# Attention in pairs of chunks: joint scores, transposes and value products ahead of two expert layers

## The chip, the core and the metric

The kernel runs on one core of one Trainium2 chip. The metric is the device time of one execution in microseconds, the median of several runs. Before the change it is 778.92 us (three runs, 778.86 to 779.86).

The engines are called as the profile calls them: PE (TensorE matmuls) and PEld (its weight loads), DVE (VectorE), ACT (ScalarE), POOL (GpSimd) and SP (SyncE, which here only issues transfers).

## What is computed

Three layers follow each other. q, k and v are 4 batches of 8 heads, 576 positions, 64 columns each.

```python
# attention over a window of 64 positions, 4 x 8 heads
scores = (1/8) * q @ k.T ; where not (0 <= i - j < 64): -1e9
x = softmax(scores) @ v                      # 2304 tokens x 512
# first MLP: 512 -> 2048 -> 512
h = x @ w_in
g = maximum(h, 0) + log1p(exp(-abs(h)))      # softplus
x = g @ w_out
# second MLP: 8 experts, each token takes the one with the largest logit
logits = x @ w_gate + modality_bias[modality_id]
out[tokens of e] = gate * (maximum(x @ w1[e], 0) @ w2[e])
```

## The kernel before

**Blocks, steps and chunks.** The 2304 tokens are cut into 6 blocks of 384. The first MLP runs over a block in 16 steps. Step f multiplies the block by the f-th 128 columns of w_in (`mm1`, lines 238 to 240: twelve matmuls, since each number is held as a high and a low part, xh and xl, and three of the four products are made), makes the softplus of it on ACT, DVE and POOL (gh and gl, its high and low parts), and two steps later (LAG is 2) multiplies gh and gl by the f-th 128 rows of w_out (`mm2`, lines 267 to 269: nine matmuls into px, three tiles of PSUM). After a block's last step ACT copies px out (`r_evac`, line 367), and in the next block DVE makes the router's dot products of it (`r_dots`, line 356).

In block 0 the weights are decoded as well (`w_decode`, lines 222 to 228): each of sixteen weight tiles W0 to W15 arrives as 64-bit numbers and is turned into two fp32r halves by two ACT and five DVE operations, two steps ahead of its use.

**Attention.** A block has 6 chunks of 64 queries. The chunks of block 0 are done ahead of the first step. The attention of block b + 1 is laid into the steps of block b, chunk by chunk, by `attn_slots` (line 184): chunk i of a block has its scores in step 2i + 1, its normalisation in step 2i + 2, its transposes in step 2i + 3 and its value products in step 2i + 4; the loads for the next chunk are in step 2i. One chunk goes this way:
- `a_scores` (line 116): 8 score matmuls of 64 x 64 x 128 into `pss` (tag pS: one tile of two PSUM banks, of which one chunk fills half); DVE adds the mask and takes the maximum, ACT makes four exponentials with their sums. Chunks under 12 (BUSY) have their mask added by 8 more matmuls.
- `a_norm` (line 151): reciprocals on DVE, the product on POOL (ACT for chunks 6 to 11).
- `a_probs` (line 161): 4 transposes into `pp` (tag pA, one bank, one buffer), copied by ACT to `pT`.
- `a_av` (line 170): 8 value matmuls into `pav` (the same tag pA), then ACT copies the result to xh and DVE takes the rest as xl. The first `mm1` of the next block reads xh and xl of all six chunks.

**What sets the order.** The program is written in the order of the loop at line 738; a scheduler then places each engine's instructions by its own estimate of time, under the data dependencies and the tiles' buffers. So what stands in a row on PE is not what stands in a row in the code. SP's transfers wait in order: a chunk's v transfer waits until the value products of the chunk two before are done.

Of the kernel before, what the change touches and what calls it, by code (L numbers as in the profile page):

```python
# [34 lines left out]
def attention_moe_moe_kernel(ctx, tc, q, k, v, w_in, w_out, modality, w_gate, mod_bias, w1, w2, out):  # L35
# [51 lines left out]
    def diff(eng, out_, a, hi):  # L87
        eng.tensor_tensor(out_, a, hi.bitcast(F32), ALU.subtract)  # L88
# [6 lines left out]
    def half(j, z):  # L95
        return (j + z) % 2
# [18 lines left out]

    def a_scores(c, tags=None, s=None):
        w = at[c]
        win, n, qT, kT = w["win"], w["n"], w["q"], w["k"]
        if tags is None:
            both = ps.tile([P, 2, 4, P], F32, name="pss", tag="pS")  # L120
            parts = [both[:, :, 0:2, 0:n]]
            bank = [both[:, z, 0:2, 0:n] for z in range(2)]
        else:
            bank = [ps.tile([P, 2, P], F32, name=f"pss{z}", tag=tags[0], bufs=tags[1])[:, :, 0:n] for z in range(2)]
            parts = [x[:, None] for x in bank]
# [34 lines left out]

    def a_probs(c, tag="pA", bufs=1, pT=None):
        s, n = at[c].pop("s"), at[c]["n"]
        pp = ps.tile([P, NPR, P], F32, name="pp", tag=tag, bufs=bufs)
        for j in range(NPR):
            nc.tensor.transpose(pp[0:n, j, :], s[:, j, 0:n], ident)
        pT = sb.tile([P, NPR, P], F32, name="pT", bufs=1) if pT is None else pT
        nc.scalar.copy(pT[0:n], pp[0:n])
        at[c]["pT"] = pT

    def a_av(c, tag="pA"):  # L170
        pT, n, vr = at[c].pop("pT"), at[c]["n"], at[c]["vr"]
        if c % CPB == 0:
            xblk[c // CPB] = (sb.tile([P, KD, TB], F32R, name="xh"), sb.tile([P, KD, TB], F32R, name="xl"))
        xh, xl = xblk[c // CPB]
        col = slice((c % CPB) * C, (c % CPB + 1) * C)
        po = ps.tile([P, NPR, C], F32, name="pav", tag=tag)
        for j in range(NPR):
            for z in range(2):
                r = slice(z * C, (z + 1) * C)
                nc.tensor.matmul(po[r, j, :], vr[0:n, j * P + z * C:j * P + (z + 1) * C], pT[0:n, 2 * z + j // 2, half(j, z) * C:(half(j, z) + 1) * C], start=True, stop=True)  # L180
        nc.scalar.copy(xh[:, :, col], po)
        diff(nc.vector, xl[:, :, col], po, xh[:, :, col])

    def attn_slots(b):

        c0 = b * CPB
        slots = [[] for _ in range(16)]
        for i in range(CPB):
            c = c0 + i
            slots[2 * i + 1].append((0, a_scores, c))  # L190
            slots[2 * i + 2].append((0, a_norm, c))
            slots[2 * i + 3].append((1, a_probs, c))
            slots[2 * i + 4].append((1, a_av, c))
            if c + 1 < B * NCB:
                slots[2 * i].append((2, a_load, c + 1))
        return slots
# [505 lines left out]
    evs = [ev0[:, i * D:(i + 1) * D] for i in range(4)] + [ev1[:, i * D:(i + 1) * D] for i in range(2)]  # L702
    work = ev1[:, 2 * D:3 * D].rearrange("p (j f) -> p j f", j=NPR)

# [3 lines left out]

    for part, c in [('qk', 0), (0, 0), ('qk', 1), ('v', 0), (1, 0), ('qk', 2), ('v', 1), ('v', 2), ('v', 3), (0, 1), ('v', 4), ('v', 5), (1, 1), (0, 2), (1, 2), ('qk', 6), ('v', 6), (0, 3), (1, 3)]:
        if part in (0, 1):  # L710
# [6 lines left out]
        else:  # L717
            a_load(c, None, part)
    for i in range(CPB + 3):
        if i < CPB:  # L720
# [7 lines left out]
        if 2 <= i < CPB + 2:  # L728
            a_probs(i - 2, "ph", 2, work if i % 2 else None)
    steps = NB * NF  # L730
# [149 lines left out]
```

## Time and profile before

| | |
|---|---|
| median of three runs | 778.92 us |
| the profiled execution's own time | 781.15 us |
| its span, first to last instruction | 779.1 us |
| mean granted clock of TensorE | 0.978 |
| PE busy, share of the span | 735.8 us, 94% |
| PEld | 617.7 us, 79% |
| DVE | 448.2 us, 58% |
| ACT | 361.6 us, 46% |
| POOL | 236.4 us, 30% |

The span falls into a beginning up to about 58 us (transfers, the attention of block 0, the first decoded weights), the rest of block 0 to about 129 us, blocks 1 to 5 to about 527 us, and the experts after it. The shares of busy time are means over these. Matmuls are pipelined: their rows overlap, so the distance from one start to the next says what a matmul costs, and not the length of its row.

### The profile page before, as it was taken

What the parts mean: (1) busy time and instruction counts of PE and PEld (TensorE: products, weight loads), DVE (VectorE), ACT (ScalarE), POOL (GpSimd) and SP (SyncE); (2) the same over time, 40 slices, a digit from 0 to 9 for tenths busy, and PEclk for the clock granted to TensorE, in tenths of its full rate; (3) what the DMA queues carried; (4) which work ended last, traced back from release to release, by engine and by line L of the source; (5) the groups of instructions that cost most, each with busy time, mean ns of one, the idle gap of its engine ahead of it and who ended that gap; (6) DMA issues with size and microseconds to landing.
All of it is one profiled execution on the core that took longest, in us unless ns stands there. A gap on an engine that the chain in (4) does not pass through costs nothing. (4 is left out here: it accounts for less than half of the span.)

```text
span 779.1 us, 12784 instructions
## 1 busy us (share of the span) xinstructions
PE 735.8 (94%) x4527; PEld 617.7 (79%) x4527; DVE 448.2 (58%) x1049; ACT 361.6 (46%) x867; POOL 236.4 (30%) x268
## 2 busy tenths in 40 slices
PE   5669999999989999999999999999989999999995
PEld 4457788888878888888788889878778888888884
DVE  6999994894397336953794349753432322223243
ACT  5779875545454445455545434543122212222143
POOL 2000000234225222333234213551464344353311
PEclk9769999999999999999999999999999999999998
DMA  9866433301141112111411015042021111111100
GB/s 329 295 212 212 155 101 122 117 1 50 36 128 42 28 48 89 35 48 49 129 36 20 23 40 200 26 178 100 17 71 50 35 56 47 37 57 43 41 28 17
DMA packets 42266, 65.17 MB, mean 84 GB/s; under 512 B 12797, under 2 KB 25469, under 8 KB 42056
## 3 DMA queue, kind: packets, MB, share of 16 engines
q1 hardware_dynamic: 37656, 54.45, 21.4%
q0 software_dynamic: 4528, 9.74, 3.8%
q8 instruction: 37, 0.61, 0.3%
q14 instruction: 45, 0.37, 0.2%
HBM read 54.37 MB, written 10.06 MB: 83 GB/s over the span
## 5 line engine op out<-in xcount | busy, mean ns | idle before, releaser
L88 POOL TENSOR_TENSOR gl<-a,gh 128x384 fp32r<-128x384 f32 x80 | 89.3, 1117 | 176.6 <-ACT gh L254 112.2
L238 PE MATMUL ph<-xh,W 128*128 128x384 f32 x384 | 133.5, 350 | 7.6 <-DVE a L251 6.1
L239 PE MATMUL ph<-xl,W 128*128 128x384 f32 x384 | 131.3, 342 | 0.8 <-DVE xl L88 0.8
L240 PE MATMUL ph<-xh,W 128*128 128x384 f32 x384 | 131.0, 341 | 0.0
L267 PE MATMUL px<-W,gh 128*128 128x512 f32 x288 | 116.3, 404 | 0.0
L268 PE MATMUL px<-W,gh 128*128 128x512 f32 x288 | 114.9, 399 | 0.0
L269 PE MATMUL px<-W,gl 128*128 128x512 f32 x288 | 107.3, 401 | 0.8 <-POOL gl L88 0.8
L249 ACT ACTIVATE a<-a 128x384 f32<-128x384 f32 x80 | 42.0, 525 | 104.2 <-DVE a L248 104.1
L159 POOL TENSOR_TENSOR s<-s,sm 128x512 f32<-128x512 f32 (+1 forms) x24 | 26.0, 1082 | 199.3 <-DVE sm L154 173.9
L238 PEld LDWEIGHTS ph<-xh,W 128*128 128x128 f32 x384 | 72.7, 190 | 15.4 <-DVE a L251 8.1
L629 POOL DMA_INDIRECT gx<-x2s,pieces x76 | 73.6, 968 | 23.6 <-issue 14.0
L239 PEld LDWEIGHTS ph<-xl,W 128*128 128x128 f32 x384 | 72.8, 190 | 4.2 <-DVE xl L88 1.5
L248 DVE TENSOR_SCALAR a<-ph 128x384 int32<-128x384 int32 x80 | 44.1, 551 | 51.6 <-PE ph L240 48.8
L251 DVE SCALAR_TENSOR_TENSOR a<-ph,a 128x384 f32<-128x384 f32 x96 | 53.0, 552 | 35.7 <-ACT a L250 35.6
L240 PEld LDWEIGHTS ph<-xh,W 128*128 128x128 f32 x384 | 73.0, 190 | 0.2
L254 ACT CAST gh<-a 128x384 fp32r<-128x384 f32 x96 | 49.0, 512 | 47.3 <-DVE a L251 45.6
L269 PEld LDWEIGHTS px<-W,gl 128*128 128x128 f32 x288 | 53.1, 188 | 13.4 <-POOL gl L88 1.7
L658 PE MATMUL p<-w,x2h 128*128 128x512 f32 x152 | 62.3, 410 | 1.2 <-ACT x2h L644 1.2
L267 PEld LDWEIGHTS px<-W,gh 128*128 128x128 f32 x288 | 54.4, 189 | 10.7 <-issue 1.2
L268 PEld LDWEIGHTS px<-W,gh 128*128 128x128 f32 x288 | 54.5, 189 | 8.9 <-issue 0.3
L661 PE MATMUL p<-w,x2h 128*128 128x512 f32 x152 | 60.4, 397 | 0.0
L662 PE MATMUL p<-w,x2l 128*128 128x512 f32 x152 | 60.3, 398 | 0.0
(196 smaller groups left out, 1335.2 us busy)
## 6 DMA issues: line engine op xcount, KB each, us to landing
raw<-in_moe_w_in_dram SPq DMA_DIRECT2D x16, 512.0 KB
raw<-in_moe_w_out_dram SPq DMA_DIRECT2D x16, 512.0 KB
r<-in_moe_w_dram SPq DMA_DIRECT2D x8, 1024.0 KB
qk<-in_k_dram SPq DMA_DIRECT2D x27, 256.0 KB
vr<-in_v_dram SPq DMA_DIRECT2D x27, 256.0 KB
qk<-in_q_dram SPq DMA_DIRECT2D x30, 128.0 KB
x2s<-xr SPq DMA_DIRECT2D x15, 256.0 KB
early<-in_v_dram SPq DMA_DIRECT2D x5, 256.0 KB
```

The costliest lines, as they stand in the source:

```text
L88: eng.tensor_tensor(out_, a, hi.bitcast(F32), ALU.subtract)
L238: nc.tensor.matmul(ph, W[f][:, 0, 0, sl], xh[:, c, :], start=c == 0, stop=False)
L239: nc.tensor.matmul(ph, W[f][:, 0, 0, sl], xl[:, c, :], start=False, stop=False)
L240: nc.tensor.matmul(ph, W[f][:, 0, 1, sl], xh[:, c, :], start=False, stop=c == KD - 1)
L251: nc.vector.scalar_tensor_tensor(a, ph, 0.0, a, ALU.max, ALU.add)
L267: nc.tensor.matmul(px[b][t], gh[:, sl], W[f][:, 1, 0, :], start=f == 0, stop=False)
L268: nc.tensor.matmul(px[b][t], gh[:, sl], W[f][:, 1, 1, :], start=False, stop=False)
L269: step["mm2"] = nc.tensor.matmul(px[b][t], gl[:, sl], W[f][:, 1, 0, :], start=False, stop=f == NF - 1)
L629: g = nc.gpsimd.indirect_dma_start(out=xr[:, c].rearrange("p c d -> p (c d)"), out_offset=None, in_=x2s[0:rows, :].rearrange("n (r f) -> ( ...
L658: first = nc.tensor.matmul(p, ah(c), bh(c), start=c == 0, stop=False)
L661: nc.tensor.matmul(p, ah(c), bl(c), start=False, stop=False)
L662: nc.tensor.matmul(p, al(c), bh(c), start=False, stop=c == n - 1)
```

## The change

From block 1's attention on (chunk 6), two chunks go through each stage together. `p_scores` gives both chunks one tile of tag pS, each its half; the matmuls, the mask, the maximum and the exponentials stay one chunk at a time. `p_probs` turns both into one tile `pp`, which is now of tag pS as well, in turn with the scores, and copies it with one ACT instruction of 128 x 1024 (two of them where a chunk is the first of its batch). `p_av` makes sixteen value products into one tile of tag pA, then one xh copy and one xl difference of 128 x 512. Pair i has its scores in step 5i, its normalisation in 5i + 1, its transposes in 5i + 3, its value products in 5i + 4; the q and k transfers of the next pair are in step 5i, its v transfers in 5i + 4. Ahead of block 0 the chunks still go one by one, with one `pT` of two halves; the first transfers of chunk 7 move up beside those of chunk 6, ahead of weight tile 3.

```diff
-    def a_scores(c, tags=None, s=None):
+    def a_scores(c, tags=None, s=None, both=None):
...
-            both = ps.tile([P, 2, 4, P], F32, name="pss", tag="pS")
-            parts = [both[:, :, 0:2, 0:n]]
-            bank = [both[:, z, 0:2, 0:n] for z in range(2)]
+            o = 2 * (c % 2) if both is not None else 0
+            both = ps.tile([P, 2, 4, P], F32, name="pss", tag="pS") if both is None else both
+            parts = [both[:, :, o:o + 2, 0:n]]
+            bank = [both[:, z, o:o + 2, 0:n] for z in range(2)]
...
+    def p_scores(c):
+        both = ps.tile([P, 2, 4, P], F32, name="pss", tag="pS")
+        for i in (c, c + 1):
+            a_scores(i, both=both)
...
+    def p_probs(c):
+        pp = ps.tile([P, 2, NPR, P], F32, name="pp", tag="pS")
+        pT = sb.tile([P, 2, NPR, P], F32, name="pT", bufs=1)
+        ns = [at[c + i]["n"] for i in range(2)]
+        for i in range(2):
+            probs_of(c + i, pp[:, i])
+            at[c + i]["pT"] = pT[:, i]
+        if ns == [P, P]:
+            nc.scalar.copy(pT, pp)
+        else:
+            for i, n in enumerate(ns):
+                nc.scalar.copy(pT[0:n, i], pp[0:n, i])
+
+    def p_av(c):
+        po = ps.tile([P, NPR, 2 * C], F32, name="pav", tag="pA")
+        for i in range(2):
+            av_of(c + i, po[:, :, i * C:(i + 1) * C])
+        put_x(c, po, 2 * C)
...
-        for i in range(CPB):
-            c = c0 + i
-            slots[2 * i + 1].append((0, a_scores, c))
-            slots[2 * i + 2].append((0, a_norm, c))
-            slots[2 * i + 3].append((1, a_probs, c))
-            slots[2 * i + 4].append((1, a_av, c))
-            if c + 1 < B * NCB:
-                slots[2 * i].append((2, a_load, c + 1))
+        for i in range(CPB // 2):
+            c = c0 + 2 * i
+            slots[5 * i].append((0, p_scores, c))
+            slots[5 * i + 1].append((0, p_norm, c))
+            slots[5 * i + 3].append((1, p_probs, c))
+            slots[5 * i + 4].append((1, p_av, c))
+            if c + 2 < B * NCB:
+                slots[5 * i].append((2, lambda c: p_load(c, "qk"), c + 2))
+                slots[5 * i + 4].append((2, lambda c: p_load(c, "v"), c + 2))
```

`probs_of`, `av_of` and `put_x` hold the transposes, the value products and the two evictions that `a_probs` and `a_av` held.

At three places the order is shown, first of the kernel before, then of the changed one. In the rows, pss are scores, pp turned probabilities, pT their copy, pav value products, ph and px the outputs of the first and the second product of the MLP, a its softplus, gh and gl the high and low part of that; numbers tell buffers apart.

PE where block 1 passes to block 2, before: the last second product of block 1, then attention, then the first matmuls that read the new xh and xl.

```order
L269 MATMUL px2_1642<-W15_1392,gl_2370 128x512
L131 MATMUL pss_2558<-qk_2413 64x128 x8
L165 MATMUL pp_2302<-ident_72,s_2200 128x128 x4
L180 MATMUL pav_2340<-pT_2307,vr_2058 64x64 x8
L131 MATMUL pss_2699<-qk_2531 64x128 x8
L238 MATMUL ph_2382<-xh_1780,W0_231 128x384
L238 MATMUL ph_2418<-xh_1780,W1_431 128x384
L239 MATMUL ph_2382<-xl_1781,W0_231 128x384
```

PE at the same passage after the change; left out are seven matmuls of the first product behind the value products, and eight of the second.

```order
L172 MATMUL pav_2292<-pT_2251,vr_1891 64x64 x8
L172 MATMUL pav_2292<-pT_2251,vr_1895 64x64 x8
L284 MATMUL ph_2313<-xh_817,W15_1361 128x384
...
L313 MATMUL px2_1649<-W13_1269,gl_2238 128x512
L132 MATMUL pss_2366<-qk_2143 64x64 x5
L282 MATMUL ph_2344<-xh_1781,W0_237 128x384
L132 MATMUL pss_2366<-qk_2143 64x64 x2
L283 MATMUL ph_2344<-xl_1782,W0_237 128x384
```

The last value products have moved ahead of the end of block 1's last first product, both chunks in a row, and the scores of the next pair stand between.

ACT at the same passage, before.

```order
L181 CAST xh_1780<-pav_2260 128x4x64
L367 COPY xr_2468<-px0_1640 128x4x4x32
L367 COPY xr_2471<-px1_1641 128x4x4x32
L148 ACTIVATE s_2449,sm_2454<-s_2449,mx_2451 128x64 x4
L367 COPY xr_2474<-px2_1642 128x4x4x32
L167 COPY pT_2307<-pp_2302 128x512
L181 CAST xh_1780<-pav_2340 128x4x64
L148 ACTIVATE s_2567,sm_2572<-s_2567,mx_2569 128x128 x4
```

ACT there after the change.

```order
L179 CAST xh_1781<-pav_2292 128x4x128
...
L149 ACTIVATE s_2375,sm_2380<-s_2375,mx_2377 128x64 x4
L298 CAST gh_2362<-a_2357 128x384
...
L411 COPY xr_2457<-px0_1647 128x4x4x32
L411 COPY xr_2460<-px1_1648 128x4x4x32
L298 CAST gh_2438<-a_2433 128x384
L411 COPY xr_2463<-px2_1649 128x4x4x32
L149 ACTIVATE s_2393,sm_2398<-s_2393,mx_2395 128x128 x4
```

The copies of px no longer have the copy of turned probabilities and xh behind them; xh has moved ahead by three steps' worth of exponentials, logarithms and gh.

DVE at the end of block 0, around the last operation of the last weight tile W15, before.

```order
L226 SCALAR_TENSOR_TENSOR raw_1259<-raw_1259 128x1024
L88 TENSOR_TENSOR gl_1332<-a_1326,gh_1331 128x384
L88 TENSOR_TENSOR W15_1392<-raw_1259,W15_1392 128x2x512
L138 TENSOR_TENSOR s_1688<-pss_1679,mask_77 128x512
L251 SCALAR_TENSOR_TENSOR a_1383<-ph_1370,a_1383 128x384
L143 TENSOR_REDUCE mx_1690<-s_1688 128x4
L88 TENSOR_TENSOR gl_1389<-a_1383,gh_1388 128x384
L144 TENSOR_SCALAR mx_1690<-mx_1690 128x4
```

DVE there after the change.

```order
L270 SCALAR_TENSOR_TENSOR raw_1266<-raw_1266 128x1024
L295 SCALAR_TENSOR_TENSOR a_1352<-ph_1339,a_1352 128x384
L88 TENSOR_TENSOR gl_1318<-a_1312,gh_1317 128x384
L154 TENSOR_SCALAR sm_1222<-sm_1222 128x4
L155 RECIPROCAL sm_1222<-sm_1222 128x4
L88 TENSOR_TENSOR W15_1361<-raw_1266,W15_1361 128x2x512
L88 TENSOR_TENSOR gl_1358<-a_1352,gh_1357 128x384
L295 SCALAR_TENSOR_TENSOR a_1403<-ph_1390,a_1403 128x384
```

The mask and maximum of chunk 13 no longer stand behind W15 (those of chunks 12 and 13 have moved behind the block), and W15 stands one softplus later.

## Rows read from the trace of the kernel before

**Rows 1.** Busy time by stretch: PE, PEld, DVE, ACT, POOL; clock, DMA share, GB/s.

```profile
60.00:92.00 32.00, 31.85 (x254) 25.25 (x253) 30.75 (x52) 30.17 (x76) 0.00 (x0) 1.00 0.62 202
...
367.00:393.00 26.00, 24.06 (x196) 19.80 (x194) 18.32 (x46) 13.44 (x37) 5.83 (x5) 1.00 0.31 97
```

**Rows 2.** Timeline of PE, a step without attention: start, length, line, tiles.

```profile
473.79 0.39 PE L267 MATMUL px<-W,gh 128*128 128x512 f32 x1
474.02 0.39 PE L268 MATMUL px<-W,gh 128*128 128x512 f32 x1
...
477.99 0.39 PE L267 MATMUL px<-W,gh 128*128 128x512 f32 x1
```

**Rows 3.** Timeline of PE, value products between two MLP matmuls.

```profile
251.53 0.40 PE L267 MATMUL px<-W,gh 128*128 128x512 f32 x1
251.86 0.69 PE L180 MATMUL pav<-pT,vr 128*64 128x64 f32 x16
252.47 0.50 PE L268 MATMUL px<-W,gh 128*128 128x512 f32 x1
252.81 0.39 PE L269 MATMUL px<-W,gl 128*128 128x512 f32 x1
```

**Rows 4.** Timeline of PE, four transposes between MLP matmuls.

```profile
257.24 0.40 PE L267 MATMUL px<-W,gh 128*128 128x512 f32 x1
257.48 0.60 PE L165 MATMUL pp<-ident,s 128*128 128x128 f32 x4
257.83 0.48 PE L268 MATMUL px<-W,gh 128*128 128x512 f32 x1
258.15 0.40 PE L269 MATMUL px<-W,gl 128*128 128x512 f32 x1
```

**Rows 5.** Timeline of PE, score matmuls of one chunk between MLP matmuls.

```profile
270.68 0.33 PE L240 MATMUL ph<-xh,W 128*128 128x384 f32 x1
270.95 0.67 PE L131 MATMUL pss<-qk 64*64 64x128 f32 x16
...
271.88 0.40 PE L268 MATMUL px<-W,gh 128*128 128x512 f32 x1
```

**Rows 6.** Timeline of PE, a piece of a score run, ahead of block 0's last first product.

```profile
126.73 0.44 PE L131 MATMUL pss<-qk 64*64 64x128 f32 x4
127.10 0.45 PE L238 MATMUL ph<-xh,W 128*128 128x384 f32 x1
```

**Rows 7.** Timeline of PE, the third first product; in brackets the idle time before.

```profile
55.06 0.44 PE L238 MATMUL ph<-xh,W 128*128 128x384 f32 x1 [2.79 <-DVE a L251]
```

**Rows 8.** Timeline of PE where blocks 1, 3 and 4 pass on.

```profile
215.19 0.66 PE L165 MATMUL pp<-ident,s 128*128 128x128 f32 x4
216.92 0.69 PE L180 MATMUL pav<-pT,vr 128*64 128x64 f32 x16 [1.07 <-ACT pT L167]
...
218.13 0.62 PE L238 MATMUL ph<-xh,W 128*128 128x384 f32 x2
219.18 0.45 PE L239 MATMUL ph<-xl,W 128*128 128x384 f32 x1 [0.43 <-DVE xl L88]
...
224.43 0.68 PE L180 MATMUL pav<-pT,vr 64*64 64x64 f32 x16 [0.67 <-ACT pT L167]
...
381.51 0.67 PE L131 MATMUL pss<-qk 64*64 64x128 f32 x16 [0.86 <-DVE s L138]
...
467.36 0.44 PE L238 MATMUL ph<-xh,W 128*128 128x384 f32 x1 [1.18 <-DVE a L251]
```

**Rows 9.** Timeline of DVE, the last operation of W15.

```profile
121.24 1.23 DVE L88 TENSOR_TENSOR W<-raw,W 128x1024 fp32r<-128x1024 f32 x1 [2.33 <-ACT W L227]
```

**Rows 10.** Groups by line and shape: count, busy us, mean ns, idle before and its releasers.

```profile
L138 DVE TENSOR_TENSOR s<-pss,mask 128x512 f32<-128x512 f32 x22 | 15.1, 687 | 17.0 <-PE pp L165 11.7 <-PE pss L131 5.2
L88 DVE TENSOR_TENSOR xl<-pav,xh 128x256 fp32r<-128x256 f32 x36 | 15.0, 417 | 12.2 <-ACT xh L181 12.2
L167 ACT COPY pT<-pp 128x512 f32<-128x512 f32 x29 | 16.9, 584 | 12.6 <-PE pp L165 12.3
```

More of the change, by code (lines that the diff above doesn't have):

```diff
@@ L159, in a_norm, with probs_of, av_of @@
             (nc.vector if c < CPB else nc.gpsimd).tensor_tensor(s[:, :, 0:n], s[:, :, 0:n], sm[:, :, None].to_broadcast((P, NPR, n)), ALU.mult)
-    def a_probs(c, tag="pA", bufs=1, pT=None):
+    def probs_of(c, pp):
         s, n = at[c].pop("s"), at[c]["n"]
-        pp = ps.tile([P, NPR, P], F32, name="pp", tag=tag, bufs=bufs)
         for j in range(NPR):
             nc.tensor.transpose(pp[0:n, j, :], s[:, j, 0:n], ident)
[L166 to L170, printed above, removed]
+    def av_of(c, po):
         pT, n, vr = at[c].pop("pT"), at[c]["n"], at[c]["vr"]
[L172 to L176, printed above, removed]
         for j in range(NPR):
@@ L180, in a_av, with put_x, a_probs, p_norm @@
                 nc.tensor.matmul(po[r, j, :], vr[0:n, j * P + z * C:j * P + (z + 1) * C], pT[0:n, 2 * z + j // 2, half(j, z) * C:(half(j, z) + 1) * C], start=True, stop=True)
+    def put_x(c, po, n):
+        if c % CPB == 0:
+            xblk[c // CPB] = (sb.tile([P, KD, TB], F32R, name="xh"), sb.tile([P, KD, TB], F32R, name="xl"))
+        xh, xl = xblk[c // CPB]
+        col = slice((c % CPB) * C, (c % CPB) * C + n)
         nc.scalar.copy(xh[:, :, col], po)
         diff(nc.vector, xl[:, :, col], po, xh[:, :, col])
+    def a_probs(c, pT):
+        n = at[c]["n"]
+        pp = ps.tile([P, NPR, P], F32, name="pp", tag="ph", bufs=2)
+        probs_of(c, pp)
+        nc.scalar.copy(pT[0:n], pp[0:n])
+        at[c]["pT"] = pT
+    def a_av(c):
+        po = ps.tile([P, NPR, C], F32, name="pav", tag="pA")
+        av_of(c, po)
+        put_x(c, po, C)
+    def p_scores(c):
+        both = ps.tile([P, 2, 4, P], F32, name="pss", tag="pS")
+        for i in (c, c + 1):
+            a_scores(i, both=both)
+    def p_norm(c):
+        for i in (c, c + 1):
+            a_norm(i)
+    def p_probs(c):
[15 more added lines that the diff above has]
+        put_x(c, po, 2 * C)
+    def p_load(c, part):
+        for i in (c, c + 1):
+            a_load(i, None, part)
     def attn_slots(b):
@@ L702, in attention_moe_moe_kernel @@
     evs = [ev0[:, i * D:(i + 1) * D] for i in range(4)] + [ev1[:, i * D:(i + 1) * D] for i in range(2)]
-    work = ev1[:, 2 * D:3 * D].rearrange("p (j f) -> p j f", j=NPR)
     def qk_load(c0, c1):
@@ L707, in qk_load @@
         nc.sync.dma_start(ek[:, c0:c1], k[0, c0:c1].rearrange("c p f -> p c f"))
-    for part, c in [('qk', 0), (0, 0), ('qk', 1), ('v', 0), (1, 0), ('qk', 2), ('v', 1), ('v', 2), ('v', 3), (0, 1), ('v', 4), ('v', 5), (1, 1), (0, 2), (1, 2), ('qk', 6), ('v', 6), (0, 3), (1, 3)]:
+    for part, c in [('qk', 0), (0, 0), ('qk', 1), ('v', 0), (1, 0), ('qk', 2), ('v', 1), ('v', 2), ('v', 3), (0, 1), ('v', 4), ('v', 5), (1, 1), (0, 2), (1, 2), ('qk', 6), ('qk', 7), ('v', 6), ('v', 7), (0, 3), (1, 3)]:
         if part in (0, 1):
@@ L718, in attention_moe_moe_kernel @@
             a_load(c, None, part)
+    pT = sb.tile([P, 2, NPR, P], F32, name="pT", bufs=1)
     for i in range(CPB + 3):
@@ L728, in attention_moe_moe_kernel @@
         if 2 <= i < CPB + 2:
-            a_probs(i - 2, "ph", 2, work if i % 2 else None)
+            a_probs(i - 2, pT[:, i % 2])
     steps = NB * NF
```

## The prediction

> **What bounds the kernel now.** I read the busy time by stretch first, then TensorE's timeline row by row, then what its idle rows name. From 60 us on TensorE hardly rests: 31.85 of the 32 us from 60 to 92 [rows 1]. A busy TensorE is only a bound if its starts stand at their closest, so look at starts: a step of the first MLP without attention (nine matmuls of the second product, twelve of the first) takes 4.20 us from one start to the same start a step later [rows 2]. The nine stand 0.23 us apart there, so the twelve (4.20 - 9 x 0.23) / 12 = 0.18. Everything above 4.20 us in a step is attention, or a stand. So I price attention by the distance of starts, not by busy time.
>
> A run of value products: 251.53 to 252.81 is 1.28 us where two plain matmuls take 0.46, so 0.82 us [rows 3]. Of that the eight products take 0.61 (251.86 to 252.47); 0.10 is the later start of the first and 0.11 the longer stay of the matmul behind it. These 0.21 us are the run's two edges. A run of four transposes costs 0.91 - 0.46 = 0.45 us, of which 0.09 is edge [rows 4]. A run of eight score matmuls costs 1.20 - 0.40 = 0.80 us, 0.20 of it edges [rows 5]. A run of two score matmuls still holds TensorE for 0.37 us before edges [rows 6], so cutting a run up is dear and joining runs is cheap.
>
> The rest is stands. At the passage from block 1 to block 2 TensorE stands three times: value products behind the copy of the turned probabilities, the first MLP matmuls behind xl, value products again [rows 8]. 215.19 to 216.92 is 1.73 us where four transposes take 0.35 (257.48 to 257.83 [rows 4]), so 1.4; 218.13 to 219.18 holds two matmuls and loses 0.7, with its edge 0.8; the bracket of 0.67 at 224.43 is 0.9 by distance. Together 3.1 us. The passage from 3 to 4 has the same three places, the first of them behind a mask addition (0.86 in brackets at 381.51): 2.6 us; the idle time of that stretch, 26.00 - 24.06 = 1.94 us in brackets [rows 1], bears that out. From 4 to 5 it stands once, 1.18 plus an edge, 1.3 us [rows 8]. Sum of the three: 7.0 us.
>
> Block 0 is different: VectorE, which also decodes the weights, is busy 30.75 of 32 us [rows 1]. The low half of the last weight tile W15 is written from 121.24 on, and the MLP step that needs it starts at 127.10 [rows 6, 9], the decode ending some 5 us ahead. So TensorE's own work sets the end of block 0, with 5 us of air to the decode.
>
> **The change part by part.** *Joint runs on TensorE.* The built order decides what is joint. I counted runs of attention matmuls between MLP matmuls. In blocks 1 to 5: before 62 runs, after 60. The value products are joint, sixteen in a row. The transposes are joint in five pairs and apart in most others. The scores of a pair are not joint: eight, then about a step of MLP, then eight. Priced with the rows above (whole score run 0.60, piece of up to five 0.36, transposes 0.35, value run 0.61, edges 0.21, or 0.09 for transposes alone):
> - before: 43 runs with scores or values 9.0, 19 of transposes alone 1.7, in them 15 score pieces 5.4, 18 score runs 10.8, transposes 8.3, values 15.9: 51.1 us;
> - after: 41 runs 8.6, 19 runs 1.7, 9 pieces 3.2, 21 score runs 12.6, transposes 8.4, 13 joint value runs at 1.19 each 15.4: 49.9 us.
>
> So -1.2 us. No row shows sixteen value products in a row: between 1.07 us (0.61 and the same again less what a run takes to come up) and 1.22 us (twice 0.61); I take 1.19, near the plain double. Range -2.8 to -0.8.
>
> *Block 0.* The same count for steps 2 to 15 gives 15.8 us before (22 runs, many of them cut up) and 11.1 after (16 runs): the new order moves the first scores of chunks 12 and 13 behind the block and joins chunks 6 and 7. Before, 0.4 us of this lies in the stand of 2.79 us ahead of the third MLP step, which waits for VectorE [rows 7]; after, 2.1 us lies there (transposes and values of chunks 6 and 7). So 15.4 against 9.0: TensorE could be 6.4 us earlier. VectorE's line up to the last softplus of the block is shorter by two mask additions and two maxima (0.69 each) and three xl (0.42 each): 4.0 us [rows 10]. With 5 us of air today I take -5.0 us, between the two. Ends: -6.4 if the air lasts, -1.0 if the decode ends only where it does now and ScalarE, shared with it, comes 4 us late.
>
> *Stands at the passages.* In the new order the last value products of a block stand inside the previous MLP step, seven MLP matmuls and nine of the second product ahead of the first matmul that reads xh: 7 x 0.18 + 9 x 0.23 = 3.3 us of cover, for an xh copy and an xl difference of 0.4 to 0.7 each. The copy of the turned probabilities (0.58 for one chunk [rows 10], about twice that for two) has seven MLP matmuls and a whole set of nine more as cover. The chains that stood are broken up: -7.0 us; at worst half comes back, -3.0. The stand late in block 5, behind gathered rows, stays: the gathers and the turning of what they bring stand as far apart as before.
>
> *New stands.* The first transposes of chunk 12 stand some 7 us behind its scores, and in between lie masks, maxima, the dot products of the router, four exponentials behind two copies, and the normalisation: about 1 us late. Elsewhere a few tenths. I take +1.5; ends +0.3 and +5 (a third of a microsecond at each of fifteen pairs).
>
> *Free edits.* Twelve copies of turned probabilities (three pairs hold a batch's first chunk and keep two), fifteen xh copies and fifteen xl differences fewer on ScalarE and VectorE cost or give nothing from block 1 on: TensorE hides them; without that cover they would give some 0.2 us each. Chunk 7's q, k and v now go ahead of the weights of tile 3 on SyncE's queue; tile 3's first ScalarE pass waits for VectorE today, not for its transfer, so I take zero. The v transfers of a pair wait for the value products of the pair before, and two weight transfers stand behind them; they are needed some three steps later: zero.
>
> Sum: -5.0 - 1.2 - 7.0 + 1.5 = -11.7 us. The profiled execution took 781.15 us (span 779.1), so 769.45; the median of the runs is 778.92, 0.29% less, so **767.3 us**. Ends, in the same measure: all low (-6.4 - 2.8 - 7.0 + 0.3 = -15.9) 763.1, all high (-1.0 - 0.8 - 3.0 + 5 = +0.2) 779.1.
>
> **The rivals.** *Decode bound (12%).* Block 0 gives nothing, because ScalarE and VectorE meet their decode rows as late as now. For it: VectorE's 30.75 of 32 us. Against it: the air of 5 us. -6.7 us, 772.2.
>
> *The passages stand as before (8%).* The three evictions of the second product and the dot products still meet the pair's softmax there. Against it: two steps between scores and transposes. -4.7 us, 774.2.
>
> *Turns on the scores' banks, slower (7%).* Before, turned probabilities had a tile of their own, shared with the value products; now they take the scores' tile in turn. TensorE then stands at each pair until both masks are added, and again until the joint copy (2 x 0.58 = 1.17 us [rows 10]) has emptied the tile. At fifteen pairs 17.5 us in place of the 1.5 I take for new stands: -13.2 + 17.5 = +4.3, by the median 783.2. It decides if more than 0.9 us per pair is exposed. Against it: between a pair's transposes and the next scores stand its value products, which need the same copy, and over 3 us of MLP. The Trainium skill, Perfetto Trace Analysis, Matmuls, says that independent groups of matmuls should rotate through different PSUM banks so that an eviction overlaps the next group; the change goes against it, and by that rule the time is this rival's. No stand of this kind is in the trace of before in the steps between passages.
>
> *Scores run jointly on the chip (4%).* The change would do all that its words say: fourteen score runs fewer in blocks 1 to 5, edges and pieces, some 4 us: 763.3. The built order speaks against it.
>
> **How the numbers follow.** Forecast 69%, rivals 12, 8, 7 and 4%. The range must reach the first two rivals and the joint scores, and may leave out the slow one and the top of the forecast's ends: 762 to 775.5. A measurement of this kernel tells 0.2% from no change, 777.4 to 780.5. Faster holds all but the slow rival and the forecast's upper end: 0.89; same 0.04; slower 0.07.
>
> **What would show it.** In the profile after: the MLP step without attention still at 4.20 us; sixteen value products in a row in about 1.2 us; no idle bracket over 0.4 us within ten steps round the passages; the last first-product step of block 0 starting near 122 us where it starts at 127.10 now. Wrong: brackets at score runs that name the copy of the turned probabilities, or at MLP matmuls of block 0 that name W.

## The result, and the profile after

The changed kernel takes 767.96 us (median of 4 runs, 766.18 to 769.55) where the kernel before took 779.39 us beside it (4 runs, 778.86 to 781.27). The ratio is 0.9848, 95% interval 0.9819 to 0.9878: 1.5% faster. Forecast were 767.3 us and a range of 762.0 to 775.5. The profiled execution of the changed kernel took 768.82 us, its span is 766.8.

To say where the 12.3 us of span went, I cut TensorE's timeline at the ends of the last first product of a block: at the start of whatever instruction stands behind the twelfth first-product matmul of steps 2, 15, 31, 47, 63, 79 and 95. Each number is a difference of two starts.

| stretch, us | before | after | difference |
|---|---|---|---|
| start to the end of step 2 | 58.38 | 58.90 | +0.5 |
| rest of block 0 | 70.94 | 64.12 | -6.8 |
| block 1 | 77.01 | 80.28 | +3.3 |
| block 2 | 84.60 | 79.48 | -5.1 |
| block 3 | 80.06 | 79.72 | -0.3 |
| block 4 | 83.75 | 79.87 | -3.9 |
| block 5 | 72.48 | 72.54 | +0.1 |
| everything behind the first MLP | 251.86 | 251.84 | 0.0 |

At each of these cuts both kernels have done the same number of second-product matmuls, but for the end of block 0: there the changed kernel has done six more, 6 x 0.23 = 1.4 us, so at equal work block 0 gains 8.2 us and block 1 loses 4.7. All of the gain lies in the first MLP, and it is not spread evenly: blocks 0, 2 and 4 gain, block 1 loses, blocks 3 and 5 stay. The first stretch of [rows 1] reads so after; below it stands the passage from block 1 to block 2, first of before, then of after (busy time by stretch; columns PE, PEld, DVE, ACT, POOL, clock, DMA share, GB/s):

```profile
60.00:92.00 32.00, 32.00 (x189) 27.96 (x188) 30.32 (x47) 27.06 (x63) 0.00 (x0) 1.00 0.50 180
203.00:229.00 26.00, 23.82 (x203) 19.66 (x203) 17.69 (x47) 12.46 (x36) 6.49 (x7) 1.00 0.37 112
200.00:226.00 26.00, 26.00 (x182) 22.24 (x181) 16.54 (x39) 12.22 (x34) 7.15 (x7) 1.00 0.23 76
```

TensorE was as busy before in the first of these stretches (31.85 us). What fell is the number of its instructions there, 254 to 189: fewer and less cut-up attention runs, some of them later. At the passage it stood 2.2 us before and does not stand at all now. What TensorE waited for between 60 us and the end of the first MLP follows, first of before, then of after (waits of PE: total, times, longest):

```profile
PE ph L238 <- DVE a L251: 3.3, 4, 1.2
PE pav L180 <- ACT pT L167: 1.7, 2, 1.1
PE pss L131 <- DVE s L138: 0.9, 1, 0.9
PE ph L239 <- DVE xl L88: 0.8, 2, 0.4
PE px L269 <- POOL gl L88: 0.8, 1, 0.8
```

```profile
PE ph L282 <- DVE a L295: 4.0, 3, 3.0
PE px L313 <- POOL gl L88: 0.3, 1, 0.3
```

The waits that [rows 8] shows at the passages (copy of the turned probabilities, mask addition, xl) are gone. One wait of 3.0 us is new; it is late in block 5.

### The profile page after: what moved, and what is told of

Same layout as the page of the kernel before. It is cut to its first block, busy times and chain, and to the rows that moved or that the text cites. A ratio compares the mean times of both kernels' runs of the same rounds, so it can differ in the third digit from the quotient of the medians.

```text
span 766.8 us, 12751 instructions
## 1 busy us (share of the span) xinstructions
PE 726.8 (95%) x4527; PEld 615.8 (80%) x4527; DVE 448.3 (58%) x1034; ACT 360.7 (47%) x840; POOL 234.8 (31%) x268
```

## The experiments

The stretches of all kernels, in the cut of the table above. In blocks 2 to 4 the nine kernels with the changed kernel's order there agree within 0.1 us, so for these blocks one profile tells. The first stretch and the last one scatter by 2.5 and by 10 us between profiled runs, whatever the kernel, and block 5 moves by up to 2.4 us with TensorE's clock (shown below), so times below are read from the stretches between, and ratios with their intervals. The cut behind block 0 holds six more second-product matmuls (1.4 us) in after, e2, e5, e9, e10 and e12 than in before, and three more (0.7 us) in e3 and e6.

| kernel | rest of block 0 | 1 | 2 | 3 | 4 | 5 | sum |
|---|---|---|---|---|---|---|---|
| before | 70.94 | 77.01 | 84.60 | 80.06 | 83.75 | 72.48 | 468.8 |
| after | 64.12 | 80.28 | 79.48 | 79.72 | 79.87 | 72.54 | 456.0 |
| e1 separate evictions | 61.97 | 82.64 | 79.55 | 79.79 | 79.81 | 71.29 | 455.0 |
| e2 pairs in block 0's MLP only | 64.13 | 77.78 | 84.95 | 80.06 | 83.75 | 72.56 | 463.2 |
| e3 pairs everywhere else | 70.47 | 76.88 | 79.48 | 79.72 | 79.87 | 72.53 | 459.0 |
| e4 before, other bank | 63.85 | 89.20 | 80.89 | 79.54 | 80.29 | 73.57 | 467.3 |
| e6 after, old bank | 71.26 | 77.09 | 82.28 | 80.02 | 78.09 | 74.32 | 463.1 |
| e7 before, scores a slot earlier | 71.22 | 77.01 | 84.12 | 79.89 | 83.33 | 72.55 | 468.1 |
| e5 rows turned later | 64.11 | 80.34 | 79.48 | 79.72 | 79.85 | 72.49 | 456.0 |
| e8 e1 and e5 | 61.95 | 83.35 | 79.55 | 79.79 | 79.81 | 72.43 | 456.9 |
| e9 gl on VectorE | 64.11 | 80.27 | 79.48 | 79.72 | 79.89 | 73.57 | 457.0 |
| e10 e5 and e9 | 64.08 | 80.21 | 79.48 | 79.72 | 79.87 | 72.46 | 455.8 |
| e11 e1, e5 and e9 | 61.97 | 83.09 | 79.55 | 79.79 | 79.81 | 70.89 | 455.1 |
| e12 after, once more | 64.13 | 80.24 | 79.48 | 79.72 | 79.87 | 73.72 | 457.2 |

My theory going in: the gain is in where the attention runs stand in TensorE's row. Rivals: the joint copies and differences carry it; the change of the bank does; only all pairs together do.

### e1: separate evictions

```diff
-        if ns == [P, P]:
-            nc.scalar.copy(pT, pp)
-        else:
-            for i, n in enumerate(ns):
-                nc.scalar.copy(pT[0:n, i], pp[0:n, i])
+        for i, n in enumerate(ns):
+            nc.scalar.copy(pT[0:n, i], pp[0:n, i])
...
-        put_x(c, po, 2 * C)
+        for i in range(2):
+            put_x(c + i, po[:, :, i * C:(i + 1) * C], C)
```

> The changed kernel, but every chunk of a pair gets copies of its own: two copies of turned probabilities, two xh copies and two xl differences in place of one each. Slots, tiles, banks and the sixteen value products in a row stay. Theory (the gain is in where the runs stand): the built order is that of the changed kernel from block 2 on, runs priced as in the prediction come to 64.0 us against 64.1, so 768 us, between 766 and 770, and TensorE waits at no new place. Rival (the joint copies carry the gain, because ScalarE and VectorE get some 0.2 us per pair and engine): fifteen pairs with three doubled copies each, up to 0.2 to 0.4 us exposed per pair, 772 to 776 us, with idle brackets of value products behind the copy of turned probabilities at most pairs.

Measured: ratio 0.9852 (0.9821 to 0.9883), as the changed kernel. Blocks 2 to 4 differ from it by 0.07, 0.07 and -0.06 us. Blocks 0 and 1 together are 0.2 us longer (144.61 against 144.40); between them the order shifts work across the cut. The joint evictions by themselves are worth nothing; TensorE hides them, as the prediction had it. Block 5 is 1.25 us shorter, which is TensorE's clock behind the late stand (shown below) and not the copies. The rival falls.

### e2 and e3: pairs in one part only

Shown is e2's edit; in e3 the condition is `b != 1`.

```diff
+    def PAIRS(b):
+        return b == 1
...
+        if PAIRS(b):
+            for i in range(CPB // 2):
...
+        else:
+            for i in range(CPB):
+                c = c0 + i
+                slots[2 * i + 1].append((0, a_scores, c))
+                slots[2 * i + 2].append((0, a_norm, c))
+                slots[2 * i + 3].append((1, s_probs, c))
+                slots[2 * i + 4].append((1, a_av, c))
```

> Pairs only for block 1's attention (chunks 6 to 11, which runs beside block 0's MLP); from chunk 12 on single chunks in the slots of the kernel before, with their turned probabilities in the bank of the value products. Theory: block 0 is shorter by 6.3 us as in the changed kernel, block 1 longer by 2 to 3 (first scores of chunks 12 and 13 come there), the stands at the passages 1 to 2, 3 to 4 and 4 to 5 are back (7.0 us); runs priced as in the prediction 67.7 us against 71.1 before. So 3.4 us under the kernel before: 776 us, between 774.5 and 777. Rival (the passage stands come from what block 0 hands on): the stands go here too and the time is under 771.

> The reverse: single chunks for block 1's attention, pairs from chunk 12 on. Theory: the passage stands are gone (7.0 us), runs in block 0 cost 19.4 us as before (19.5), runs in all 67.4 against 71.1, the late stand in block 5 is 2.2 us longer as in the changed kernel, small new stands 1: 779.4 - 7.0 - 3.7 + 3.2 = 772 us, between 769 and 774. With the run of pairs in block 0 alone the two losses against the changed kernel should add up: (this - 768) + (pairs in block 0 alone - 768) near 11.4 us. Rival (the gain is one thing that needs all pairs): each half alone gives under 2 us, both above 777.

Measured: e2 0.9948 (0.9930 to 0.9967), e3 0.9876 (0.9839 to 0.9913). By the sums of the table e2 is 5.6 us under the kernel before and e3 9.9, together 15.5 us where the whole change gives 12.8; by the ratios it is 4.1 and 9.7 us, together 13.7 against 11.9. So each part gives something by itself, and the rival that needs all pairs falls. But the parts do not simply add up: by the sums 2.7 us are lost when both are in, of which 2.5 lie in block 1 (77.78 us in e2, 80.28 in the changed kernel); by the ratios it is 1.8, within their intervals. e2 has block 0's -6.8 and, in blocks 2 to 5, the stretches of before within 0.4 us, with their waits. e3 has blocks 2 to 5 of after within 0.02 us and block 0 of before within 0.5 us (1.2 at equal work). The stands at the passages owe nothing to what block 0 hands on. e3 gave 2.4 us more than the 7.5 us expected; which term of the expectation that was is not settled. TensorE's one wait in e3 between 60 us and the end of the MLP is the late one.

### e4 and e6: the bank without pairs, pairs without the bank

e4 is the kernel before with the turned probabilities of one chunk in the scores' tile:

```diff
-    def a_probs(c, tag="pA", bufs=1, pT=None):
+    def a_probs(c, tag="pS", bufs=1, pT=None):
```

> The kernel before with one word changed: the turned probabilities of a single chunk go to the scores' tile instead of the value products' bank. No pairs, no joint copies, the slots of before. Its built order differs: 13 runs in block 0 where 24 stood, runs priced at 65.7 us against 71.1 before and 64.1 in the changed kernel. Theory (what counts is how the runs are cut up and where they stand, and pairs are one way to get there): runs alone give -5.4 us, the passages keep single chunks and about half of their 7.0 us of stands, so 770 to 774, 772 us. Rival 1 (only pairs help, by their joint copies and longer distance): 777 to 780. Rival 2 (turns on the scores' bank cost a stand at each chunk, as the prediction's slow rival says): 0.5 us or more at 30 chunks, 785 us and above, with score runs waiting for the copy of turned probabilities.

e6 is the changed kernel with them in the value products' bank:

```diff
-        pp = ps.tile([P, 2, NPR, P], F32, name="pp", tag="pS")
         pT = sb.tile([P, 2, NPR, P], F32, name="pT", bufs=1)
-        ns = [at[c + i]["n"] for i in range(2)]
         for i in range(2):
-            probs_of(c + i, pp[:, i])
+            n = at[c + i]["n"]
+            pp = ps.tile([P, NPR, P], F32, name="pp", tag="pA")
+            probs_of(c + i, pp)
+            nc.scalar.copy(pT[0:n, i], pp[0:n])
             at[c + i]["pT"] = pT[:, i]
```

> The changed kernel with the turned probabilities back in the value products' bank: one chunk at a time, each copied before the other chunk of the pair may be turned; slots, scores' tile, joint value products and joint xh and xl stay. Its built order cuts the runs up again: priced as in the prediction 69.2 us against 64.1 in the changed kernel, 19.5 of them in block 0 (14.1). Theory (the order of the runs carries the gain): the MLP's last step ends 5 us later than in the changed kernel, near 520 us (518 to 523), ratio 0.991. Rival 1 (each turn of the one bank costs a stand of a copy's length, 0.6 us, at fifteen pairs): 9 us more, 529 us, ratio 1.003. Rival 2 (the pairs as such carry it, whatever the bank): 515 us, 0.985.

Measured: e4 0.9950 (0.9929 to 0.9971), e6 0.9911 (0.9880 to 0.9943), its last MLP step ending at 521.59 us. e6 fits the theory. e4's ratio makes 775.5 us of the kernel before's 779.4, 1.5 us above the theory's range and as far below the first rival's. Together with before and after they make a square (block 0 at equal work, that is less the 1.4 and 0.7 us named above):

| us | bank of the value products | bank of the scores |
|---|---|---|
| single chunks: rest of block 0; blocks 2 and 4 | 70.9; 168.35 | 63.9; 161.18 |
| pairs: rest of block 0; blocks 2 and 4 | 70.6; 160.37 | 62.7; 159.35 |

Block 0's shorter time belongs to the bank: -7.1 and -7.8 us with it, -0.4 and -1.1 with pairs. Part of that is work moved behind the cut: over blocks 0 and 1 together the bank gives 3.9 us with pairs (148.35 to 144.40), and with single chunks it costs 5.1 (147.95 to 153.05). Blocks 2 and 4 are cured by either, -7.2 by the bank, -8.0 by pairs, -9.0 by both. What then separates e4 from the changed kernel, 467.3 against 456.0, is block 1: 8.9 of 11.3 us, 7.5 at equal work. The rows say why (timeline of PE, then of DVE, at the passage into block 1 in e4):

```profile
136.50 0.64 PE L165 MATMUL pp<-ident,s 128*128 128x128 f32 x4
137.82 0.69 PE L180 MATMUL pav<-pT,vr 128*64 128x64 f32 x16 [0.69 <-ACT pT L167]
142.29 0.69 PE L238 MATMUL ph<-xh,W 128*128 128x384 f32 x1 [3.78 <-DVE a L251]
142.78 0.52 PE L239 MATMUL ph<-xl,W 128*128 128x384 f32 x1
143.10 0.52 PE L240 MATMUL ph<-xh,W 128*128 128x384 f32 x1
```

```profile
141.07 0.69 DVE L356 SCALAR_TENSOR_TENSOR prod<-xr,wga 128x512 f32<-128x512 f32 x1 [3.81 <-DMA wga<-wgd]
141.68 0.08 DVE L356 DVE_READ_ACCUMULATOR prod<-xr,wga 128x1 f32 x1
141.68 0.55 DVE L251 SCALAR_TENSOR_TENSOR a<-ph,a 128x384 f32<-128x384 f32 x1
```

TensorE names the softplus, and the softplus stands in VectorE's line behind a dot product that waits 3.81 us for the router's weights. In e4's built order the transposes that prepare these weights (L337) stand at the passage, behind step 15's products; in the changed kernel they stand in step 12. By distance the stand is 3.9 us and the one behind the copy ahead of it 1.0. During the long stand TensorE's clock fell: from 142 to 146 us the granted clock is 0.50, its lower level of 1.2 GHz, and the first products start 0.32 us apart where 0.18 is plain. From 142.29 to 147.58 that is some 2.4 us, so 7.3 us in all; the changed kernel has 1.9 us of stands of its own in this block. By these rows e4 falls short because its order starts a transfer too late, and because the clock falls behind the stand. No run with the transfer earlier tests it. Turns on the scores' bank are not the reason: TensorE waits for a copy of turned probabilities twice in e4 from 60 us on, 2.4 us in all, and never in the changed kernel. So here sharing the scores' bank costs no stand per chunk and none per pair.

### e7: single chunks with a step more between scores and transposes

```diff
-            slots[2 * i + 1].append((0, a_scores, c))
-            slots[2 * i + 2].append((0, a_norm, c))
+            slots[2 * i].append((0, a_scores, c))
+            slots[2 * i + 1].append((0, a_norm, c))
```

> The kernel before, single chunks, with scores and normalisation of each chunk one slot earlier, so that a step more lies between scores and transposes, as in the changed kernel. Runs priced as in the prediction 71.7 us against 71.1. Theory as the prediction put it (the passages are cured because a step more lies between scores and transposes): the 7.0 us of stands at the passages go, 0.6 comes back, the MLP's last step ends near 521 us where the kernel before has 527.2; ratio 0.992. Rival (the stands come from how many runs the built order packs into the two steps at a passage, and that is the same here: transposes, scores and values of three chunks between steps 32 and 34): within 1.5 us of 527, ratio 0.998 to 1.002, with value products behind the copy of turned probabilities near 216 us.

Measured: ratio 0.9980 (0.9964 to 0.9996); last MLP step's end 526.70 us. The rival holds. The passage from block 1 to block 2 (timeline of PE; the places of [rows 8]):

```profile
215.97 0.66 PE L165 MATMUL pp<-ident,s 128*128 128x128 f32 x4
217.36 0.69 PE L180 MATMUL pav<-pT,vr 128*64 128x64 f32 x16 [0.73 <-ACT pT L167]
...
219.48 0.45 PE L239 MATMUL ph<-xl,W 128*128 128x384 f32 x1 [0.29 <-DVE xl L88]
```

Transposes, their copy, values, xl and the product that reads it still follow one another, with a score run between them at most; blocks 2 and 4 lose 0.9 us of the 5.7 that stand at their passages [rows 8]. A slot number sets when a piece may go, not where it lands. The passage is nearly cured where the built order spreads these pieces (from 200 to 230 us TensorE waits 0.6 us in e4, 0.4 in e6 and never after), and stands where it packs them (2.1 us before, 1.2 in e7). e6 keeps the stand from block 4 to block 5, 1.2 us.

### e5, e8, e9, e10, e11, e12: the stand late in block 5

After, the last wait of any size is this (timeline of PE, of DVE, of POOL):

```profile
506.25 0.44 PE L282 MATMUL ph<-xh,W 128*128 128x384 f32 x1 [3.02 <-DVE a L295]
```

```profile
502.77 0.71 DVE L684 STREAM_TRANSPOSE x2T<-gx 128x512 f32<-128x512 f32 x1 [4.22 <-DMA gx<-x2s,pieces]
503.41 2.32 DVE L88 TENSOR_TENSOR w<-r,w 128x1024 fp32r<-128x1024 f32 x2
505.64 0.55 DVE L295 SCALAR_TENSOR_TENSOR a<-ph,a 128x384 f32<-128x384 f32 x1
```

```profile
505.72 0.95 POOL L673 DMA_INDIRECT gx<-x2s,pieces  x1 [0.30 <-issue]
506.69 1.98 POOL L88 TENSOR_TENSOR gl<-a,gh 128x384 fp32r<-128x384 f32 x2
```

By the distance of starts steps 94 and 95 take 7.43 and 5.80 us, less 2 x 4.20: 4.8 us above plain. Before, the same place cost 5.63 + 5.34 - 8.40 = 2.6 us, and there one gl went ahead of the last gather:

```profile
510.37 1.88 POOL L629 DMA_INDIRECT gx<-x2s,pieces  x1 [0.30 <-issue]
512.27 1.14 POOL L88 TENSOR_TENSOR gl<-a,gh 128x384 fp32r<-128x384 f32 x1
513.57 1.23 POOL L629 DMA_INDIRECT gx<-x2s,pieces  x1 [0.15 <-issue]
```

Not all of the 4.8 us is the stand. Behind it TensorE's clock fell, by a different amount in each profiled execution (busy time by stretch, the clock third from the end: after, e12, e11):

```profile
505.00:515.00 10.00, 8.75 (x37) 8.01 (x38) 6.27 (x7) 3.43 (x7) 5.36 (x6) 0.83 0.61 208
505.00:515.00 10.00, 8.23 (x27) 7.46 (x28) 6.77 (x8) 3.53 (x7) 5.39 (x6) 0.66 0.55 182
505.00:515.00 10.00, 7.02 (x35) 6.00 (x34) 4.47 (x9) 3.83 (x8) 3.27 (x4) 1.00 0.52 168
```

From 508 to 511 us the granted clock of after and of e12 is 0.50, which is 1.2 GHz, and first products start 0.32 us apart. e1 has the wait of after, 3.02 us for the same softplus, and a granted clock of 1.00 throughout; its steps 94 and 95 take 6.76 and 5.22 us, 3.6 above plain. So 1.2 of the 4.8 us is the lower clock. All of block 5 goes by it in the nine kernels with the changed kernel's order: 71.29 and 70.89 us where the mean from 505 to 515 us is 1.00 (e1, e11), 72.43 to 72.54 where it is 0.83 (after, e3, e5, e8, e10), 73.57 and 73.72 where it is 0.66 (e9, e12). At equal clock no edit below moved block 5 by more than 0.4 us. Before, no such fall is on the trace, so its 2.6 us are to be held against the 3.6 of e1 and the 3.2 of e11.

e5 moves the turning of the gathered rows behind the softplus of step 14; e9 moves three gl differences to VectorE; e10 does both; e8 and e11 have separate evictions besides; e12 is the changed kernel beside e9 to e11.

```diff
+            if f == 14:
+                x_turn(("e", 0), step["sp", last, 14])
...
-                x_turn(("e", 0))
```

```diff
-        diff(nc.gpsimd if b else nc.vector, gl, a, gh)
+        diff(nc.gpsimd if b and (b < NB - 1 or f not in (12, 13, 14)) else nc.vector, gl, a, gh)
```

> The changed kernel with one instruction later in VectorE's line: the turning of the first gathered rows (it waits 4.2 us for them, 498.6 to 502.8) stands behind the softplus of the step after next instead of ahead of one. Theory (VectorE's queue behind that wait is what TensorE stands for at steps 94 and 95, 4.9 us above plain): the first product of the MLP's last step ends 3.4 to 4.9 us sooner, 510.0 to 511.5 us from the start where the changed kernel has 514.9, and the ratio to the kernel before is 0.980. Rival (GpSimd's line: its gl differences stand behind eight gathers until 506.7): the stand stays, 513.5 to 515 us, and the ratio is 0.984 to 0.985.

> The changed kernel with separate evictions per chunk (its last MLP step ended at 513.6 us, the changed kernel's at 514.9) and the later turning of the gathered rows in one. Theory: both gains add up, since one lies in block 0 and the other at steps 94 and 95: 513.6 less 2.5 to 3.5, so 510.1 to 511.1 us, ratio 0.979. Rival (GpSimd's gathers hold the late stand): 513 us and more, ratio 0.983 to 0.985.

> The changed kernel with the gl difference of the last block's steps 12, 13 and 14 on VectorE instead of GpSimd, so that no gl stands behind the gathers. The turning of the gathered rows stays where it is, and VectorE waits for them as before. Theory (two queues hold the late stand, each enough by itself): the stand stays, from the passage into block 5 to the end of its MLP 71 to 72.6 us where the changed kernel takes 72.5; ratio to the kernel before 0.983 to 0.985. Rival (GpSimd's line alone holds it): 67.5 to 69 us, ratio 0.979.

> The changed kernel with both: the gl differences of steps 12, 13 and 14 on VectorE, and the turning of the gathered rows behind the softplus of step 14. Theory (two queues): the late stand goes, from the passage into block 5 to the end of its MLP 67.6 to 68.6 us where the changed kernel and each of the two edits alone take 72.5; ratio to the kernel before 0.979 to 0.981. Rival (a third line, ScalarE's halving of weights or VectorE's own, holds it too): 70 us or more, ratio 0.982 or above.

> As the one before, and separate evictions per chunk as in the first experiment (whose last MLP step ended 1.3 us sooner than the changed kernel's). Theory: the gains are in different stretches and add up as far as the first is more than the scatter of the start: last MLP step's end 509 to 510.5 us, ratio 0.978 to 0.980. Rival (the 1.3 us were scatter, the copies cost nothing and give nothing): within 0.5 us of the kernel before it in this list.

> The changed kernel itself, on the same chip as the three others, for a direct comparison: ratio 0.9848 as measured, its last MLP step ending at 514.9 us or, where block 0's first weights arrive later, up to 1.5 us after that, all of it ahead of block 0's third step. Every difference of the three others from it that lies outside block 0's first steps and steps 92 to 95 would be scatter.

Measured ratios: e5 0.9848 (0.9819 to 0.9878), e8 0.9848 (0.9806 to 0.9890), e9 0.9848 (0.9820 to 0.9877), e10 0.9828 (0.9805 to 0.9851), e11 0.9793 (0.9763 to 0.9822), e12 0.9855 (0.9830 to 0.9880). Block 5: 72.49, 72.43, 73.57, 72.46, 70.89 and 73.72 us. So e5 and e8 went with their rival (e5's last step ends 1.0 us behind the rival's range, as its start took 1.1 us longer). e9 stays at the stretch of the changed kernel beside it, both about 1 us above the bound I gave, where the clock is 0.66. e10, meant to settle the matter, gave what I had put down for a third line. The rows of e10 name that line (waits of PE from 480 to 515 us; timeline of POOL; of DVE):

```profile
PE px L313 <- POOL gl L88: 3.0, 1, 3.0
```

```profile
491.22 1.99 POOL L88 TENSOR_TENSOR gl<-a,gh 128x384 fp32r<-128x384 f32 x2
...
505.82 0.94 POOL L673 DMA_INDIRECT gx<-x2s,pieces  x1 [0.30 <-issue]
506.78 1.00 POOL L88 TENSOR_TENSOR gl<-a,gh 128x384 fp32r<-128x384 f32 x1
```

```profile
510.46 0.70 DVE L684 STREAM_TRANSPOSE x2T<-gx 128x512 f32<-128x512 f32 x1
```

VectorE no longer waits for the rows, and TensorE stands as long for another reason: a gl on GpSimd, behind eight gathers, at 506.78. One gl was left there: behind the pair at 491.22 it is the only one, and the edit took those of steps 12, 13 and 14 away, so it is that of step 11. My edit began one step too late, in e9 as in e10, so e9 does not tell the two lines apart either. What this shows: the wait in VectorE's line can be taken away without any gain (e5), and GpSimd's line is long enough to hold the stand. What it leaves open: whether the stand goes once step 11's gl is moved too. That was not run.

e11 is the fastest kernel of this study, and e12 beside it was slower (771.43 us against 777.47; their intervals do not meet). Its ratio lies in the theory's range. Its last step ends 0.4 us ahead of e10's, and so it goes with the rival. In the spans of the profiled executions it is 3.5 us under e12 (772.98 against 776.52): 0.6 in the first stretch, 0.9 in the last, 2.1 between them. Of these, block 5 gives 2.8 and blocks 0 and 1 take 0.7 back, and what block 5 gives goes with the clock: 1.00 in e11 and 0.66 in e12, behind a wait of 3.0 us in both. e8, with the same evictions and a clock of 0.83, has 72.43 there. e1, at a clock of 1.00 like e11, has 71.29, so at equal clock the traces show 0.4 us for e11's edits; the rest of the 6 us between the medians is in executions that have no trace. e12 against after is the same case: block 5 takes 1.2 us longer with the same instructions, by the clock, against my expectation of no difference outside the start.

## Why the prediction was right

*The prices.* A plain step is 4.21 us after (starts 64.24 and 68.45). Sixteen value products in a row take 1.08 us; I took 1.19 and had 1.07 as the lower end. Eight joint transposes take 0.79 to the next start, where I had 0.70. The joint copy takes 1.01, not 1.17 (timeline of PE between MLP matmuls, then a group by line and shape):

```profile
169.55 1.03 PE L165 MATMUL pp<-ident,s 128*128 128x128 f32 x8
170.34 0.42 PE L282 MATMUL ph<-xh,W 128*128 128x384 f32 x1
...
200.63 0.34 PE L283 MATMUL ph<-xl,W 128*128 128x384 f32 x1
200.90 1.15 PE L172 MATMUL pav<-pT,vr 128*64 128x64 f32 x32
201.98 0.44 PE L284 MATMUL ph<-xh,W 128*128 128x384 f32 x1
```

```profile
L212 ACT COPY pT<-pp 128x1024 f32<-128x1024 f32 x12 | 12.1, 1012 | 1.8 <-PE pp L165 1.7
```

*Block 0: -5.0 taken, -6.3 measured at its end* (129.33 to 123.02, the start counted in). At equal work it is -7.7, more than the -6.4 of the count, part of which only moved on: block 1 is 4.7 longer at equal work, in part runs that the prediction had in its count for blocks 1 to 5, in part the new stands below. I held back 1.4 for the decode, and it was not needed: the decode moved along (timeline of DVE, then of PE, last tile and last step of block 0):

```profile
117.28 1.23 DVE L88 TENSOR_TENSOR W<-raw,W 128x1024 fp32r<-128x1024 f32 x1 [0.57 <-ACT W L271]
```

```profile
119.08 0.34 PE L282 MATMUL ph<-xh,W 128*128 128x384 f32 x1
```

The row of [rows 9] stood at 121.24; it went forward by 4.0 us, which is the 4.0 us I had counted off VectorE's line, and ended 0.57 us ahead of the first matmul of the last step. The air of 5 us was spent nearly whole, and no bracket in this stretch names W. I forecast that the step would start near 122; it starts at 119.08 and, with its second products and transposes in between, ends at 123.02. The decode-bound rival (12%) falls.

*Blocks 1 to 5: -1.2 - 7.0 + 1.5 = -6.7 taken, -6.0 measured.* Block 3, whose stretch holds none of the passages that stood before, shows nearly the joint runs alone: -0.3 us. Blocks 2 and 4, which did, gain 5.1 and 3.9. Into block 5 the stand of 1.3 [rows 8] is gone too, and the late stand, with the lower clock behind it, took it back. So the rival in which the passages stand as before (8%) falls, and the one with joint scores (4%) too: after, the scores of a pair stand apart by some second products of the MLP or more, as built. The new stands are where I looked for them and of the size taken: chunk 12's transposes hold TensorE for 135.88 - 134.86 = 1.02 us, 0.67 above [rows 4], 0.76 follow at step 19 and 0.45 at step 26, 1.9 in all against 1.5 (timeline of PE):

```profile
134.86 0.66 PE L165 MATMUL pp<-ident,s 128*128 128x128 f32 x4
135.88 0.44 PE L282 MATMUL ph<-xh,W 128*128 128x384 f32 x1 [0.37 <-DVE a L295]
...
140.93 0.45 PE L282 MATMUL ph<-xh,W 128*128 128x384 f32 x1 [0.58 <-DVE a L295]
```

The second bracket is over the 0.4 us that I had set as the limit round a passage; both name the softplus, which stands behind the router's dot products in VectorE's line.

*What failed, though the sum came out.* Three steps. That the forecast lies 0.7 us from the measured time is luck to the extent that their errors cancel.

First, "the stand late in block 5 stays". It grew from 2.6 to 4.8 us, +2.2, about half of it the lower clock behind it. I had reasoned that gathers and their turning stand as far apart as before; what the rows show changed is how GpSimd's gl stand among the gathers, a queue that I did not look at there. That these gl hold the stand is read from rows, as no run took all of them away. Block 0's extra -1.3 and the passages covered for it.

Second, the reason for the passages. I wrote that the chains break up because two steps lie between scores and transposes. e7 has that distance in its slots with single chunks, and 0.9 us of the 5.7 in blocks 2 and 4 went. What breaks the chains is the order that is built, and either the bank or the pairs change it.

Third, the turns on the scores' bank. The prediction carried it only as a cost, with 7% for 17.5 us. No such stand is in the trace: the largest bracket of after is at a first-product matmul, none at a score run. The Trainium skill, Perfetto Trace Analysis, Matmuls, wants independent matmul groups on rotating banks. Here the bank is shared without such a stand, and over 3 us of MLP lie between the two uses. e4 and e6 show the move to be the gain of block 0 itself, -7.1 and -7.8 us, of which part comes back in block 1. So the term of block 0 has the right mechanism (fewer pieces, work moved behind the block) and nearly the right size, and the prediction put the wrong part of the change behind it: it spoke of chunks joined and moved by the new order, and the order is new because of the bank.

## What to carry to other kernels

Price a change by distances of starts and cut the time into stretches at the same instructions: here the middle blocks repeat to a tenth of a microsecond while the whole run scatters by 1%, and a sum that comes out hides two errors of 2 us that the stretches show. Where a scheduler builds the order, a tile's bank also decides what may stand where: moving one temporary to another bank rearranged a whole block here, so test bank and batching apart before crediting either. A wait that is removed from one queue gives nothing while a second queue holds the same consumer; read the queue of every engine at such a place and move all of the work that stands behind the long transfer, from its first item on (this last was not run here). Read the granted clock behind every stand before two kernels are compared: here it moved block 5 by 1.2 to 2.4 us behind the same wait of 3.0 us.

## What was not expected of the hardware

With the same instructions the stretch behind the first MLP took 251.84 us in one profiled execution of the changed kernel and 259.88 in another. Of the 8.0 us between them 5.5 are one wait, of a transpose for an h that stands behind ScalarE's reading of a register (timeline of PE, after and e12):

```profile
561.14 0.65 PE L726 MATMUL pth<-ident,h 128*128 128x128 f32 x4 [1.37 <-ACTq L695]
```

```profile
568.29 1.12 PE L726 MATMUL pth<-ident,h 128*128 128x128 f32 x4 [6.89 <-ACTq L695]
```

Most of the rest is the clock behind that wait: from 569 to 574 us the granted clock of e12 is 0.50 (1.2 GHz), and its matmuls of 512 columns start 0.43 us apart where 0.23 is plain. The long wait is 5.8 to 7.2 us in all eight kernels of e1 to e4 and e9 to e12, beside which the kernel before took 787.9 and 788.1 us; it is 1.4 us at most in the six others, beside which that took 779.4 and 780.3. So it goes with the occasion and not with an edit. Why is not settled here.

And VectorE's dot product, 0.69 us by itself, takes 1.28 us in one place where GpSimd scales probabilities at the same time (timeline of DVE, then of POOL, after):

```profile
132.80 0.69 DVE L400 SCALAR_TENSOR_TENSOR prod<-xr,wga 128x512 f32<-128x512 f32 x1
...
134.07 1.28 DVE L400 SCALAR_TENSOR_TENSOR prod<-xr,wgb 128x512 f32<-128x512 f32 x1
```

```profile
133.76 1.04 POOL L160 TENSOR_TENSOR s<-s,sm 128x512 f32<-128x512 f32 x1 [126.95 <-DVE sm L155]
```

Not every overlap does this. In after the 70 dot products that no work of GpSimd overlaps take 0.68 to 0.69 us, and the 46 that it overlaps by over 0.1 us take 0.68 to 1.39.
